# The operands of a Strassen-like second layer for the next pair of token blocks: made in the first layer and read back from DRAM

## The chip, the core and the metric

The kernel runs on one core of a Trainium2 chip. A core has a matrix engine (TensorE, PE in the profile; its weight loads are PEld), three engines for elementwise work (VectorE is DVE, ScalarE is ACT, GpSimd is POOL) and a queue that issues DMAs (SyncE, SP). Each engine runs its instructions in order and waits at semaphores for the others. The metric is the device time of one execution in microseconds; smaller is better. The profiled times come from one execution that was recorded.

## What is computed

Attention without softmax, an RMS norm over each head, a first feed-forward layer with a maximum of three products, an RMS norm, and a gated second layer:

```python
kv = np.einsum('bhsd,bhse->bhde', k, v)
out = np.einsum('bhsd,bhde->bhse', q, kv)              # 8 x 8 heads x 576 x 64
x = (out / rms(out) * g_norm) -> (4608, 512)
h = np.maximum(np.maximum(x @ w1, x @ w2), x @ w3)     # 512 -> 768
x = h @ w_out                                          # 768 -> 512
xn = x / rms(x) * rms_g
g = xn @ w_gate                                        # 512 -> 1536
return (silu(g) * (xn @ w_val)) @ w_out2               # 1536 -> 512
```

All in fp32, and the weights come as 64-bit floats.

## The kernel before

*Precision.* A product of fp32 matrices is made of three matmuls (`mm3`, `prod3`): each operand is split into a high part (an ACT copy to the matrix engine's fp32 format) and a low part (the difference, on DVE or POOL), and high x high, high x low and low x high are added up. Every operand that PE reads therefore costs one ACT and one DVE or POOL operation first.

*First layer.* The 4608 tokens are 9 blocks `t` of 512. The loop over `t` = 2 to 8 runs six steps `j`, one for each 128 of the 768 columns: `do_p` makes three products into PSUM; ACT copies the first ("s"), DVE takes the maximum with the second ("s", line 323) and the third ("h", line 327), and the result is split ("hs"). `do_o` adds it into the four accumulators of the output. Between the products, `mid` calls `pump`, which moves on the conversion of the weights from 64-bit floats: `store_pair` converts, sums, splits and stores the second layer's weights in DRAM ("ws" to "wd"). The attention of the next block ("ao", "pk", "pt") also runs in these steps. After a block, `end1` copies the accumulators to four tiles "y", and `end1_rest`, moved on by one call of `flush` a step, norms them and stores them in DRAM as `xn_d[t]`. All temporaries of 512 columns come from one pool "t" of 8 buffers (`tmp`).

*Second layer.* One block (`NB`) is done in the plain way (`do_gv`, "the gated part", six matmuls by two halves for each of 12 steps). The other eight form four pairs `n`, and a pair is multiplied by a scheme with 7 products in place of 8 (as Strassen and Winograd do it). It has 3 phases of 4 units each (`run_unit`; a unit is the gate, i = 0, or the value, i = 1, for 256 columns), and at a phase's end `down` multiplies by the output weights. The products m = 1, 2, 3 take blocks of the input as they are; m = 5, 6, 4, 7 take sums and differences of blocks. Each of the 7 has two halves k, so a pair needs 14 split operands, "xo".

`build_x` makes them: it starts in the last unit of a pair's third phase for the next pair and goes on through `down`, one step in every second `slot`. The raw blocks "xr" are loaded a phase earlier (`load_x`). The differences run on DVE (`diff`, line 491), the high parts on ACT (line 483), the low parts in turn on POOL, POOL and DVE (line 486). `consume` takes a product out of PSUM: the sum "c" on DVE, then the sigmoid "sg" on ACT and its product "sl" on DVE, two ticks later (`defer`; `tick` follows each product). Weights come through `Ring`, four loads ahead, on SP; the buffers of operands and weights ("u", 38) are shared.

The order of work on each engine is that of the program text, with the deferred calls at their ticks; no scheduler moves it.

Of the kernel before, what the change touches and what calls it, by code (L numbers as in the profile page):

```python
# [34 lines left out]
def tile_kernel(ctx: ExitStack, tc, qT, k, v, gcol, w1, w2, w3, wo, wg, wv, wo2, rmsg, out):  # L35
# [89 lines left out]
    def store_pair(i, jp):  # L125
# [27 lines left out]
        for n, src in enumerate((quarters[0], c0, c1, quarters[1])):  # L153
            g = unit([P, 2, 2, 256], F32R, "ws")
            for o, (dst, sv) in enumerate([(g, src)] if n in (1, 2) or i < 2 else [(g[:, k], src[k]) for k in range(2)]):
                if isinstance(sv, tuple):
                    sv = (t0, t1)[n // 2]
                hi, lo = (dst[:, 0], dst[:, 1]) if len(dst.shape) == 3 else (dst[:, :, 0], dst[:, :, 1])
                nc.scalar.activation(hi, sv, AF.Copy)
                nc.vector.tensor_tensor(lo, sv, f32(hi), ALU.subtract)  # L160
            d = w_d[i, jp, n] = dp.tile([P, 2, 2, 256], F32, name="wd", tag=f"wd{i}_{jp}_{n}")
            nc.sync.dma_start(d, f32(g))
            yield
# [5 lines left out]

    def pump(n=1):  # L170
        for _ in range(n):
            for g in list(flight):
                if next(g, 0) == 0:
                    flight.remove(g)
            if todo and len(flight) < most[0]:
                start(todo[0])
# [230 lines left out]
    def end1_rest(t, y, q, w):  # L407
# [20 lines left out]
        for c in range(KC):  # L428
            nc.sync.dma_start(xn_d[t][c * P:(c + 1) * P, :], y[c])

# [42 lines left out]
    def load_x(t):  # L473
        raw = xp.tile([P, KC, 2, TB], F32, tag="x", name="xr")
        for k in range(2):
            nc.sync.dma_start(raw[:, :, k], xn_d[t + k].rearrange("(c p) n -> p c n", p=P))
        XR.append(raw)

    n_lo = [0]

    def split_b(key, src):
        x = unit([P, 2, TB], F32R, "xo")
        nc.scalar.activation(x[:, 0], src, AF.Copy)  # L483
        n_lo[0] += 1
        eng = nc.vector if n_lo[0] % 3 == 0 else nc.gpsimd
        eng.tensor_tensor(x[:, 1], src, f32(x[:, 0]), ALU.subtract)  # L486
        XO[key] = x

    def diff(x, y, name):
        t = tmp(name)  # L490
        nc.vector.tensor_tensor(t, x, y, ALU.subtract)  # L491
        return t

    def build_x():
        raw = XR.pop(0)
        b11, b12, b21, b22 = ([raw[:, 2 * r + k, c] for k in range(2)] for r in range(2) for c in range(2))
        t1, t2 = {}, {}
        for k in range(2):
            split_b((1, k), b11[k])
        yield  # L500
        for k in range(2):
            t1[k] = diff(b12[k], b11[k], "t1")
            split_b((5, k), t1[k])
        yield
        for k in range(2):
            split_b((2, k), b21[k])
        yield
        for k in range(2):
            t2[k] = diff(b22[k], t1[k], "t2")
            split_b((6, k), t2[k])  # L510
        yield
        for k in range(2):
            split_b((3, k), b22[k])
        yield
        for k in range(2):
            split_b((7, k), diff(b22[k], b12[k], "t3"))
        yield
        for k in range(2):
            split_b((4, k), diff(b21[k], t2[k], "t4"))
# [95 lines left out]
    def hidden(jp, c, h):  # L615

        HQ[jp, c] = h

        def part(m, src):
            HO[jp, m] = split_h(src, "ho")  # L620

        if c == 0:
            defer(lambda: part(1, h))
        elif c == 1:
            t1 = T[jp, 1] = diff(h, HQ[jp, 0], "t1")
            defer(lambda: part(5, t1), 1)
        elif c == 3:
            t2 = T[jp, 2] = diff(h, T.pop((jp, 1)), "t2")
            t3 = diff(h, HQ[jp, 1], "t3")
            defer(lambda: part(6, t2))  # L630
            defer(lambda: part(3, h), 5)
            defer(lambda: part(7, t3), 7)
        else:
            t4 = diff(h, T.pop((jp, 2)), "t4")
            defer(lambda: part(2, h), 1)
            defer(lambda: part(4, t4), 5)


    def consume(u, c, p, s=None):
        n, jp, i = u["key"]  # L640
        src = p if s is None else add(p, s, tmp("c"))
        if i == 0:
            sg = tmp("sg")
            nc.scalar.activation(sg, src, AF.Sigmoid)  # L644

            def mult():
                sl = small("sl")
                nc.vector.tensor_tensor(sl, src, sg, ALU.mult)
                SL[c] = sl

            defer(mult)
# [55 lines left out]
    def down(n, ph, xs):  # L707
# [25 lines left out]
        def put(d, c, p, alone=False):  # L733
            o = place(d, c)
            if ph + 1 == NPH:
# [3 lines left out]
                nc.sync.dma_start(out[r:r + P, q:q + TB], t)  # L739
# [36 lines left out]
        for d in range(2):  # L776
            prod_down(d, ph, 4, acc[d][0])
            put(d, 2, acc[d][0], True)
            slot()
        if xs is not None:  # L780
            for _ in xs:
                pass

    with tc.manual_schedule():
# [13 lines left out]
        for i in range(2):  # L798
            z = unit([P, 2, NP, P], F32, "kvbd")
            nc.gpsimd.memset(z, 0.0)  # L800
            kvb += [z[:, 0], z[:, 1]]
# [39 lines left out]
        def kv_upto(need, ahead=True):  # L841
            while n_kv[0] <= min(need, B - 1):
                n = n_kv[0]
                do_kv(n, kvb[n % 4])
# [121 lines left out]
        for j in range(J2):  # L966
# [8 lines left out]
            do_gv(NB, j, none)  # L975
            if 3 <= j <= 5:
                flush()
# [9 lines left out]
            if j == 2:  # L987
                xb = build_x()
# [5 lines left out]
        for _ in xb:  # L994
            pass
        for n in range(NPAIR):
            for ph in range(NPH):
                more = n + 1 < NPAIR
                xs = None
                for jp in range(PPH * ph, PPH * (ph + 1)):  # L1000
                    for i in range(2):
                        if i == 1 and jp + 1 == PPH * (ph + 1):
                            load_down(ph)
                            if ph + 1 == NPH and more:
                                xs = build_x()
# [40 lines left out]
```

## Time and profile before

| | |
|---|---|
| median of 3 runs | 1582.43 us (1580.74 to 1583.18) |
| the profiled execution's own time | 1582.51 us |
| span of the profiled execution | 1580.4 us |
| PE busy | 1500.0 us, 95% of the span |
| DVE, ACT, POOL busy | 953.1, 580.1, 490.5 us (60%, 37%, 31%) |
| mean granted clock of PE | 0.978 of full speed |
| moved by DMA | 278 MB, 176 GB/s over the span |

The first layer takes up about 700 us, the gated part lasts until about 835 us, and each of the 12 phases of the second layer is some 58 us of matmuls. A row of the timeline gives the start, the duration, the engine, the source line, the operation with its output and inputs, and in brackets how long the engine had been idle before and for whom. Matmuls overlap: a matmul of 512 columns is listed with about 390 ns while six of them start within 1.36 us. A granted clock of 1.00 is 2.4 GHz, 0.50 is 1.2 GHz.

### The profile page before, as it was taken

The page shows a single profiled execution, that of the slowest core. Times are in us where ns is not written, and L with a number is a line of the kernel's source. Part 1 is how long each engine was busy: PE and PEld are TensorE (multiplying, and loading weights), DVE is VectorE, ACT ScalarE, POOL GpSimd, SP SyncE. Part 2 cuts the span into 40 slices and gives each one's busy share as a digit, 9 for nine tenths or more (in the row PEclk, how much of TensorE's full clock was granted, in tenths as well). Part 3 has the DMA queues.
Part 4 walks back from the last instruction along what each step waited for, and adds up shares of the span by engine and source line. Part 5 has one row for each costly group of instructions (what it writes and reads, how often), then busy time and mean ns, then how long its engine had stood idle before and what let it go on. Part 6 is the DMA issues. An engine that isn't in the chain of part 4 may idle for free. (4 is left out here: it accounts for less than half of the span.)

```text
span 1580.4 us, 19695 instructions
## 1 busy us (share of the span) xinstructions
PE 1500.0 (95%) x7200; PEld 1230.8 (78%) x7200; DVE 953.1 (60%) x1404; ACT 580.1 (37%) x1027; POOL 490.5 (31%) x375
## 2 busy tenths in 40 slices
PE   5899999999989999999999999799988999899998
PEld 5787878787778878888887878588776887678887
DVE  4875565656666567642525476764676655865656
ACT  3443333434343434322324334243243432434422
POOL 2543222212222222211422242532343422544323
PEclk8999999999999999999999999899998999999999
DMA  9322437354724353446428474184543854456442
GB/s 305 121 67 81 119 115 260 127 169 151 255 98 160 135 199 135 173 149 260 178 86 318 162 270 170 60 326 180 220 160 121 308 200 157 161 206 246 161 169 104
DMA packets 117343, 278.11 MB, mean 176 GB/s; under 512 B 10496, under 2 KB 41216, under 8 KB 117248
## 3 DMA queue, kind: packets, MB, share of 16 engines
q1 hardware_dynamic: 117248, 276.87, 48.6%
q8 instruction: 57, 0.93, 0.2%
q14 instruction: 38, 0.31, 0.1%
HBM read 220.20 MB, written 56.62 MB: 175 GB/s over the span
## 5 line engine op out<-in xcount | busy, mean ns | idle before, releaser
L292 PE MATMUL p<-x,w 128*128 128x512 f32 (+1 forms) x652 | 262.2, 402 | 17.6 <-DVE h L327 12.8
L293 PE MATMUL p<-x,w 128*128 128x512 f32 (+1 forms) x652 | 257.7, 395 | 0.4 <-DVE x L285 0.3
L294 PE MATMUL p<-x,w 128*128 128x512 f32 (+1 forms) x652 | 257.2, 394 | 0.0
L582 PE MATMUL ua<-xo,w 128*128 128x512 f32 x864 | 215.5, 392 | 8.0 <-ACT s L659 8.0
L582 PEld LDWEIGHTS ua<-xo,w 128*128 128x128 f32 x864 | 161.9, 188 | 46.5 <-ACT s L659 13.1
L311 POOL TENSOR_TENSOR ho<-sl,ho 128x512 fp32r<-128x512 f32 x72 | 100.3, 1401 | 308.3 <-issue 163.2
L311 POOL TENSOR_TENSOR hs<-h,hs 128x512 fp32r<-128x512 f32 x54 | 69.6, 1289 | 383.9 <-ACT hs L310 305.7
L311 POOL TENSOR_TENSOR ho<-t,ho 128x512 fp32r<-128x512 f32 x96 | 131.5, 1374 | 135.7 <-ACT ho L310 123.6
L292 PEld LDWEIGHTS p<-x,w 128*128 128x128 f32 x652 | 125.7, 193 | 46.4 <-DVE h L327 14.2
L582 PE MATMUL ub<-xo,w 128*128 128x512 f32 x576 | 146.3, 389 | 0.0
L294 PEld LDWEIGHTS p<-x,w 128*128 128x128 f32 x652 | 125.5, 192 | 26.4
L293 PEld LDWEIGHTS p<-x,w 128*128 128x128 f32 x652 | 125.7, 193 | 25.5 <-DVE x L285 1.0
L582 PEld LDWEIGHTS ub<-xo,w 128*128 128x128 f32 x576 | 108.1, 188 | 22.7
L582 PE MATMUL da<-ho,wd 128*128 128x512 f32 x432 | 109.8, 398 | 4.9 <-DVE op L612 3.4
L310 ACT ACTIVATE hs<-h 128x512 fp32r<-128x512 f32 x54 | 34.1, 632 | 193.8 <-DVE h L327 184.4
L659 ACT ACTIVATE s<-ua 128x512 f32<-128x512 f32 x96 | 57.2, 596 | 123.1 <-PE ua L582 122.8
L582 PEld LDWEIGHTS da<-ho,wd 128*128 128x128 f32 x432 | 82.8, 193 | 24.5 <-DVE op L612 4.7
L310 ACT ACTIVATE ho<-t 128x512 fp32r<-128x512 f32 x96 | 59.3, 627 | 100.8 <-DVE t L491 100.8
L256 POOL TENSOR_TENSOR rs<-ms,mhalf 128x8 f32<-128x8 f32 x36 | 61.9, 1725 | 109.0 <-DVE ms L254 106.1
L644 ACT ACTIVATE sg<-c 128x512 f32<-128x512 f32 x72 | 45.5, 632 | 108.3 <-DVE c L612 108.3
L292 PE MATMUL acc<-hs,w 128*128 128x512 f32 x216 | 84.9, 393 | 0.0
L582 PE MATMUL db<-ho,wd 128*128 128x512 f32 x288 | 74.7, 398 | 10.4 <-ACT ho L310 6.5
(133 smaller groups left out, 2733.8 us busy)
## 6 DMA issues: line engine op xcount, KB each, us to landing
w<-wd SPq DMA_DIRECT2D x180, 512.0 KB, 7.7
wd<-ws SPq DMA_DIRECT2D x72, 512.0 KB, 3.1
wd<-wd SPq DMA_DIRECT2D x72, 512.0 KB, 6.5
wq<-wd SPq DMA_DIRECT2D x72, 256.0 KB, 7.7
raw<-in_w SPq DMA_DIRECT2D x18, 512.0 KB, 8.2
q<-in_qT SPq DMA_DIRECT2D x18, 512.0 KB, 6.0
raw<-in_wo SPq DMA_DIRECT2D x18, 512.0 KB, 6.3
xn<-y SPq DMA_DIRECT2D x36, 256.0 KB, 3.1
```

The costliest lines, as they stand in the source:

```text
L256: nc.gpsimd.tensor_tensor(rs, ms, mhalf.to_broadcast([P, H]), ALU.pow)
L292: nc.tensor.matmul(o, ah, bh, start=first, stop=False)
L293: nc.tensor.matmul(o, ah, bl, start=False, stop=False)
L294: nc.tensor.matmul(o, al, bh, start=False, stop=last)
L310: nc.scalar.activation(hs[:, 0], h, AF.Copy)
L311: nc.gpsimd.tensor_tensor(hs[:, 1], h, f32(hs[:, 0]), ALU.subtract)
L582: nc.tensor.matmul(o, aa, bb, start=first and q == 0, stop=last and q == 2, skip_group_check=True)
L644: nc.scalar.activation(sg, src, AF.Sigmoid)
L659: nc.scalar.activation(t, p, AF.Copy)
```

## The change

For each pair, `pair_sums` makes the eight operands that are sums (m = 5, 6, 4, 7, two halves) out of the tiles "y" of the second block of the pair, which are still there, and the first block's blocks read back from `xn_d[t - 1]`. It splits them and stores high and low part in DRAM ("td"). It is queued in `side` when an even block has been stored and moved on twice by each `pump` (and by the gated part's steps). `build_x` then loads these eight and makes only the six others, with all low parts on POOL; `load_x` reads three of four quarters. In `consume` the sigmoid is a deferred call, and so is the store of an output in `put`. A weight's store in `store_pair` comes a step later, the block matrices "kvbd" have two buffers in place of four, and the last `flush` calls come a step earlier.

```diff
@@ store_pair, pump
+            yield
             d = w_d[i, jp, n] = dp.tile([P, 2, 2, 256], F32, name="wd", tag=f"wd{i}_{jp}_{n}")
             nc.sync.dma_start(d, f32(g))
-            yield
...
+    def aside():
+        if side and next(side[0], 0) == 0:
+            side.pop(0)
+
     def pump(n=1):
         for _ in range(n):
+            aside()
+            aside()
             for g in list(flight):
@@ end1_rest
             nc.sync.dma_start(xn_d[t][c * P:(c + 1) * P, :], y[c])
+        if t and t % 2 == 0:
+            side.append(pair_sums(t, y))
@@
+    def pair_sums(t, y):
+
+        n = t // 2 - 1
+
+        def put(m, k, src):
+            hi = tmp("th").bitcast(F32R)
+            nc.scalar.activation(hi, src, AF.Copy)
+            nc.vector.tensor_tensor(src.bitcast(F32R), src, f32(hi), ALU.subtract)
+            return m, k, hi, src
+
+        def store(m, k, hi, lo):
+            d = t_d[n, m, k] = dp.tile([P, 2, TB], F32, name="td", tag=f"td{n}_{m}_{k}")
+            nc.sync.dma_start(d[:, 0], f32(hi))
+            nc.sync.dma_start(d[:, 1], lo)
+
+        for k in range(2):
+            b12, b22 = y[k], y[2 + k]
+            b11, b21 = tmp("b11"), tmp("b21")
+            for b, c in ((b11, k), (b21, 2 + k)):
+                nc.sync.dma_start(b, xn_d[t - 1][c * P:(c + 1) * P, :])
+            yield
+            yield
+            t1 = diff(b12, b11, b11)
+            t2 = diff(b22, t1, tmp("t2"))
+            yield
+            p1 = put(5, k, t1)
+            t4 = diff(b21, t2, b21)
+            yield
+            store(*p1)
+            p1 = put(6, k, t2)
+            yield
+            store(*p1)
+            p1 = put(4, k, t4)
+            t3 = diff(b22, b12, tmp("t3"))
+            yield
+            store(*p1)
+            p1 = put(7, k, t3)
+            yield
+            store(*p1)
...
+    def build_x(n):
+
         raw = XR.pop(0)
-        b11, b12, b21, b22 = ([raw[:, 2 * r + k, c] for k in range(2)] for r in range(2) for c in range(2))
...
+        for m, r in ((1, 0), (5, None), (2, 1), (6, None), (3, 2), (7, None), (4, None)):
+            for k in range(2):
+                x = unit([P, 2, TB], F32R, "xo")
+                if r is None:
+                    nc.sync.dma_start(f32(x), t_d[n, m, k])
+                else:
+                    nc.scalar.activation(x[:, 0], raw[:, r, k], AF.Copy)
+                    nc.gpsimd.tensor_tensor(x[:, 1], raw[:, r, k], f32(x[:, 0]), ALU.subtract)
+                XO[m, k] = x
+            yield
@@ consume, put, down
-            sg = tmp("sg")
-            nc.scalar.activation(sg, src, AF.Sigmoid)
-
-            def mult():
+            def gate():
+                sg = tmp("sg")
+                nc.scalar.activation(sg, src, AF.Sigmoid)
+                defer(lambda: mult(sg))
+
+            def mult(sg):
                 sl = small("sl")
                 nc.vector.tensor_tensor(sl, src, sg, ALU.mult)
                 SL[c] = sl
 
-            defer(mult)
+            if s is None:
+                gate()
+            else:
+                defer(gate, 1)
...
-                nc.sync.dma_start(out[r:r + P, q:q + TB], t)
+                defer(lambda: nc.sync.dma_start(out[r:r + P, q:q + TB], t), 1)
...
+        tick()
```

What this does to the order on the engines, at three places. First DVE in the first layer, t = 3, from the attention's "xn" in step j = 3 to the maximum "s" of j = 4. Before ("wt" are weights in conversion):

```order
L261 TENSOR_TENSOR xn<-po,rs 128x512
L107 TENSOR_SCALAR wt<-wt 128x512
L108 SCALAR_TENSOR_TENSOR wt<-raw,wt 128x512
L109 ISA wt<-wt 128x1024
L99 TENSOR_SCALAR wt<-raw 128x512
L323 TENSOR_TENSOR s_2888<-p_2875,s_2866 128x512
```

After; "b" and "t" are the differences of `pair_sums` (L486), "th" their high parts (L496 is the low part):

```order
L269 TENSOR_TENSOR xn<-po,rs 128x512
L486 TENSOR_TENSOR b_2846<-y,b_2846 128x512
L486 TENSOR_TENSOR t_2871<-y,b_2846 128x512
L496 TENSOR_TENSOR b_2846<-b_2846,th 128x512
L486 TENSOR_TENSOR b_2847<-b_2847,t_2871 128x512
L107 TENSOR_SCALAR wt<-wt 128x512
L108 SCALAR_TENSOR_TENSOR wt<-raw,wt 128x512
L109 ISA wt<-wt 128x1024
L99 TENSOR_SCALAR wt<-raw 128x512
L331 TENSOR_TENSOR s_2897<-p_2884,s_2868 128x512
```

Four of the sixteen operations stand ahead of this "s"; the others follow in the same way up to the end of j = 5.

Second, DVE in the last units of the first pair's third phase, before, from the last "t" of one value unit to the first sum of the last unit:

```order
L491 TENSOR_TENSOR t_8135<-sl,t_8061 128x512
L648 TENSOR_TENSOR sl<-c,sg 128x512
L612 TENSOR_TENSOR c<-ua,s_8088 128x512
L648 TENSOR_TENSOR sl<-c,sg 128x512
L486 TENSOR_TENSOR xo<-xr,xo 128x512
L612 TENSOR_TENSOR c<-uc,s_8182 128x512
```

and after:

```order
L486 TENSOR_TENSOR t_8383<-sl,t_8309 128x512
L641 TENSOR_TENSOR c<-ua,s_8336 128x512
L679 TENSOR_TENSOR sl<-c,sg 128x512 x2
L641 TENSOR_TENSOR c<-uc,s_8430 128x512
L688 TENSOR_TENSOR sl<-c,sl 128x512
```

The sum "c<-ua", on which the next sigmoid waits, has moved ahead of one product "sl", and the subtraction of "xo" has left DVE.

Third, SP at the end of that phase. Before, "w" and "wq" are weights of the next units, "wd" and the "wq" of line 562 those of `down`, and "out" the output stores:

```order
L565 DMA wd<-wd 128x1024 x6
L562 DMA wq<-wd 128x512 x2
L546 DMA w<-wd 128x1024 x3
L543 DMA wq<-wd 128x512
L546 DMA w<-wd 128x1024
L739 DMA out<-o 128x512 x8
```

and after, with the loads of operands from "td" between them:

```order
L594 DMA wd<-wd 128x1024 x6
L591 DMA wq<-wd 128x512 x2
L575 DMA w<-wd 128x1024 x2
L543 DMA xo<-td 128x1024 x2
L575 DMA w<-wd 128x1024
L572 DMA wq<-wd 128x512
L575 DMA w<-wd 128x1024
L543 DMA xo<-td 128x1024 x2
L773 DMA out<-o 128x512 x2
L543 DMA xo<-td 128x1024 x2
L773 DMA out<-o 128x512
L543 DMA xo<-td 128x1024 x2
```

Five more output stores follow. The eight loads stand between weights and stores, in four pairs.

## Rows read from the trace of the kernel before

**Rows 1.** The page, part 1: busy us, share of the span, instructions of each engine.
```profile
PE 1500.0 (95%) x7200; PEld 1230.8 (78%) x7200; DVE 953.1 (60%) x1404; ACT 580.1 (37%) x1027; POOL 490.5 (31%) x375
```

**Rows 2.** Waits of PE: line, for whom, us in total, times, longest us.
```profile
PE p L292 <- DVE h L327: 12.8, 7, 2.8
...
PE da L582 <- DVE o L612: 8.7, 3, 4.1
PE ua L582 <- ACT s L659: 8.0, 12, 0.7
```

**Rows 3.** Timeline of the first build (start, us, engine, line, operation, idle before).
```profile
982.97 1.65 PE L582 MATMUL ua<-xo,w 128*128 128x512 f32 x6 [0.67 <-ACT s L659]
...
993.63 0.63 ACT L310 ACTIVATE ho<-t 128x512 fp32r<-128x512 f32 x1 [3.19 <-DVE t L491]
...
994.31 0.79 PE L582 MATMUL db<-ho,wd 128*128 128x512 f32 x1 [3.56 <-ACT ho L310]
...
997.12 2.76 PE L582 MATMUL ua<-xo,wq 128*128 128x512 f32 x6
...
1018.63 5.49 PE L582 MATMUL da<-ho,wq 128*128 128x512 f32 x12 [3.24 <-DVE o L612]
...
1023.91 1.70 PE L582 MATMUL ua<-xo,w 128*128 128x512 f32 x6
```

**Rows 4.** Windows there: stretch, its us, busy us (instructions), clock, DMA share, GB/s.
```profile
984.00:994.00 10.00, 6.75 (x30) 5.25 (x28) 9.13 (x10) 3.72 (x7) 6.40 (x4) 0.98 0.11 43
994.00:1000.00 6.00, 4.69 (x10) 3.42 (x11) 5.01 (x8) 2.42 (x5) 4.37 (x4) 0.50 0.01 3
```

**Rows 5.** Groups of instructions, DVE differences: busy us, mean ns, idle before.
```profile
L491 DVE TENSOR_TENSOR t<-sl 128x512 f32<-128x512 f32 x48 | 34.8, 725 | 1.7
...
L491 DVE TENSOR_TENSOR t<-xr 128x512 f32<-128x512 f32 x16 | 20.4, 1301 | 0.0
```

**Rows 6.** Timeline of the last phase, which builds nothing.
```profile
1549.85 1.67 PE L582 MATMUL ua<-xo,w 128*128 128x512 f32 x6 [0.67 <-ACT s L659]
...
1562.44 2.54 POOL L311 TENSOR_TENSOR ho<-sl,ho 128x512 fp32r<-128x512 f32 x2 [1.70 <-PE db L582]
...
1573.89 2.88 PE L582 MATMUL da<-ho,wq 128*128 128x512 f32 x12
```

**Rows 7.** Timeline of PE in the second and third build.
```profile
1173.28 1.66 PE L582 MATMUL ua<-xo,w 128*128 128x512 f32 x6 [0.67 <-ACT s L659]
...
1214.79 1.82 PE L582 MATMUL ua<-xo,w 128*128 128x512 f32 x6
...
1364.28 1.66 PE L582 MATMUL ua<-xo,w 128*128 128x512 f32 x6 [0.67 <-ACT s L659]
...
1372.07 0.73 PE L582 MATMUL da<-ho,wd 128*128 128x512 f32 x2 [1.15 <-POOL ho L311]
...
1400.67 1.52 PE L582 MATMUL ua<-xo,w 128*128 128x512 f32 x6
```

**Rows 8.** DMA issues: count, KB each, median us from issue to landing.
```profile
w<-wd SPq DMA_DIRECT2D x180, 512.0 KB, 7.7
```

**Rows 9.** Timeline of DVE and ACT ahead of the wait at 982.97.
```profile
979.33 1.77 DVE L648 TENSOR_TENSOR sl<-c,sg 128x512 f32<-128x512 f32 x1
...
981.03 0.68 DVE L612 TENSOR_TENSOR c<-ua,s 128x512 f32<-128x512 f32 x1
...
981.80 0.63 ACT L644 ACTIVATE sg<-c 128x512 f32<-128x512 f32 x1 [3.54 <-DVE c L612]
982.34 0.58 ACT L659 ACTIVATE s<-ua 128x512 f32<-128x512 f32 x1
```

**Rows 10.** Windows in the first layer and the gated part: PE, PEld, DVE, ACT, POOL.
```profile
333.00:366.00 33.00, 33.00 (x217) 27.49 (x216) 18.12 (x35) 11.85 (x23) 4.66 (x5) 1.00 0.59 205
...
743.00:821.00 78.00, 78.00 (x346) 64.48 (x345) 33.00 (x43) 20.64 (x36) 26.53 (x20) 1.00 0.45 174
```

**Rows 11.** Timeline of PE in the first layer, a stop for "h".
```profile
396.77 0.79 PE L292 MATMUL p<-x,w 128*128 128x512 f32 x1 [2.76 <-DVE h L327]
```

**Rows 12.** A window of the first layer with a full DMA.
```profile
348.00:358.00 10.00, 10.00 (x45) 8.27 (x45) 3.95 (x7) 2.63 (x6) 0.00 (x0) 1.00 1.01 335
```

**Rows 13.** Waits of the queue SP.
```profile
SPq L546 <- PE da L582: 118.9, 24, 14.7
```

More of the change, by code (lines that the diff above doesn't have):

```diff
@@ L168, in start @@
         flight.append(g)
+    side = []
+    def aside():
+        if side and next(side[0], 0) == 0:
+            side.pop(0)
     def pump(n=1):
         for _ in range(n):
+            aside()
+            aside()
             for g in list(flight):
@@ L471, in tile_kernel @@
     HO = {}
[L473 to L487, printed above, removed]
@@ L489, in diff @@
-    def diff(x, y, name):
-        t = tmp(name)
+    t_d = {}
+    def diff(x, y, t):
         nc.vector.tensor_tensor(t, x, y, ALU.subtract)
         return t
-    def build_x():
-        raw = XR.pop(0)
-        b11, b12, b21, b22 = ([raw[:, 2 * r + k, c] for k in range(2)] for r in range(2) for c in range(2))
[L497 to L519, printed above, removed]
+    def pair_sums(t, y):
[33 more added lines that the diff above has]
+            store(*p1)
@@ new lines, in load_x @@
+    def load_x(t):
+        raw = xp.tile([P, 3, 2, TB], F32, tag="x", name="xr")
+        nc.sync.dma_start(raw[:, 0], xn_d[t][:2 * P].rearrange("(c p) n -> p c n", p=P))
+        for k in range(2):
+            nc.sync.dma_start(raw[:, 1 + k], xn_d[t + k][2 * P:].rearrange("(c p) n -> p c n", p=P))
+        XR.append(raw)
+    def build_x(n):
+        raw = XR.pop(0)
+        for m, r in ((1, 0), (5, None), (2, 1), (6, None), (3, 2), (7, None), (4, None)):
+            for k in range(2):
+                x = unit([P, 2, TB], F32R, "xo")
[6 more added lines that the diff above has]
+            yield
@@ L624, in hidden @@
         elif c == 1:
-            t1 = T[jp, 1] = diff(h, HQ[jp, 0], "t1")
+            t1 = T[jp, 1] = diff(h, HQ[jp, 0], tmp("t1"))
             defer(lambda: part(5, t1), 1)
         elif c == 3:
-            t2 = T[jp, 2] = diff(h, T.pop((jp, 1)), "t2")
-            t3 = diff(h, HQ[jp, 1], "t3")
+            t2 = T[jp, 2] = diff(h, T.pop((jp, 1)), tmp("t2"))
+            t3 = diff(h, HQ[jp, 1], tmp("t3"))
             defer(lambda: part(6, t2))
@@ L633, in hidden @@
         else:
-            t4 = diff(h, T.pop((jp, 2)), "t4")
+            t4 = diff(h, T.pop((jp, 2)), tmp("t4"))
             defer(lambda: part(2, h), 1)
@@ L797, in tile_kernel @@
         kvb = []
[L798 to L801, printed above, removed]
+        z = unit([P, 2, NP, P], F32, "kvbd")
+        nc.gpsimd.memset(z, 0.0)
+        kvb += [z[:, 0], z[:, 1]]
         nc.sync.dma_start(gc, gcol)
@@ L843, in kv_upto @@
                 n = n_kv[0]
-                do_kv(n, kvb[n % 4])
+                do_kv(n, kvb[n % 2])
                 n_kv[0] += 1
@@ L974, in tile_kernel @@
                 wr.load(1)
-            do_gv(NB, j, none)
-            if 3 <= j <= 5:
+            do_gv(NB, j, aside)
+            aside()
+            if 2 <= j <= 4:
                 flush()
@@ L987, in tile_kernel @@
             if j == 2:
-                xb = build_x()
+                xb = build_x(0)
             if j > 2 and xb is not None:
@@ L995, in tile_kernel @@
             pass
+        while side:
+            aside()
         for n in range(NPAIR):
@@ L1004, in tile_kernel @@
                             if ph + 1 == NPH and more:
-                                xs = build_x()
+                                xs = build_x(n + 1)
                         run_unit(n, jp, i, xs)
```

## The prediction

> **What bounds the kernel now.** I read the page first: the matrix engine (PE) is busy for 95% of the span, DVE for 60%, ACT for 37%, POOL for 31% [rows 1]. So PE is the bound, and a change that leaves its 7200 matmuls as they are can only take back time in which PE waits, or add to it. The waits of PE come next [rows 2]. Three families matter: 8.0 us in 12 waits for a copy "s" of ACT, at most 0.7 us each, one in every phase of the second layer; waits of "da" and "db" in the three phases that also build the operands of the next pair, of which the one for DVE "o" is the largest; and 12.8 us of "p" for DVE "h" in the first layer, into which the change puts work.
>
> Then the timeline of the first of the three building phases [rows 3]: PE stops for 3.56 us, later for 3.24 us, and after each stop it is slow: six matmuls take 2.76 us, where twelve take 2.88 us at full clock; the granted clock of 994 to 1000 us is 0.50, that is 1.2 instead of 2.4 GHz [rows 4]. So a stop costs more than its length. DVE is the late one: busy for 9.13 of the 10 us before and in the first long stop [rows 4], and ACT, whose split PE waits for, waited 3.19 us itself for a DVE difference [rows 3]. A difference of the build costs DVE 1.301 us on the mean, where POOL works beside it, one of the unit's own 0.725 us [rows 5].
>
> **The change part by part.**
>
> *The builds lose their DVE work.* Each of the three late builds has 8 differences and 4 or 5 of its 14 subtractions on DVE, and 8 of its 14 ACT copies belong to sums. All these go, and 8 loads of 512 KB from DRAM replace them. I price the stretch against the one phase with the same products and stores and no build, the last of the program: from its wait for "s" at 1549.85 to the end of its last products, 1573.89 + 2.88, it takes 26.92 us [rows 6]. The builds take, up to the next pair's first product, 1023.91 - 982.97 = 40.94 us [rows 3], 1214.79 - 1173.28 = 41.51 and 1400.67 - 1364.28 = 36.39 us [rows 7]. Over 26.92 that is 14.02 + 14.59 + 9.47 = **38.1 us** to be had, the low clock's share included.
>
> Not all of it, since six ACT copies and six POOL subtractions stay in each build. Two stand on POOL ahead of the splits that the first "da" needs; the third build already has that order, and "da" waited 1.15 us for POOL there [rows 7]. Two more stand ahead of the two splits that "dc" needs. In the phase without a build POOL is idle for 1.70 us before those, and two such operations take 2.54 us [rows 6], so "dc" comes 0.8 us later. Bounds: nothing, or both pairs in full, 2 x 2.54 = 5.1 us a build. I take 0.7 (POOL is faster once DVE's differences are gone) and 0.8, so **4.5 us** of the three stay.
>
> *The loads* stand on SP, in order, among the weights of the next pair and the output stores. A load that waits for a free buffer holds what is behind it. A 512 KB load of weights lands 7.7 us after its issue [rows 8]. The two last pairs of loads (m = 7 and 4) go out during the last four groups of twelve matmuls, some 11 us before the pair ends, and the next pair wants m = 7 only five products, about 7 us, after its start, m = 4 a unit later. DMA is busy for 11% before the first stop [rows 4]. I cost the loads at nothing, hidden behind those products; the third rival is the case without that cover.
>
> *The gates.* The sigmoid is deferred by one tick, but that tick follows at once, so on ACT it keeps its place. What moves is DVE's product "sl", by one matrix product, since its two ticks are now counted from the sigmoid: in the phase's last but one unit "c<-ua" stands ahead of a "sl<-c,sg" instead of behind it. What that is worth: the product takes 1.77 us, only then comes "c", "sg" has left ACT idle for 3.54 us, and the copy that PE waits for stands behind "sg" [rows 9]. With "c" first, "sg" runs some 1.7 us earlier, more than the 0.67 us of the wait. All twelve should go: **8.0 us** [rows 2], or nothing if it is the order on ACT that makes them.
>
> *The sums made early.* Per pair there are 8 differences and 8 subtractions on DVE, 8 copies on ACT, 4 loads and 16 stores of 256 KB on SP, within about 33 us: for three pairs in the steps j = 3 to 5 of t = 3, 5 and 7, for the last pair in the gated part. There PE has no gap in 743 to 821 us and DVE is busy for 33.00 of 78 us [rows 10], part of it the old first build, which goes; I cost this pair at nothing. In 333 to 366 us, the place in t = 3 (t = 5 and 7 repeat it), PE has no gap either and DVE is busy for 18.12 of 33 us [rows 10]. Sixteen operations at 0.725 us [rows 5] are 11.6 us; 14.9 us are free. By the sum they fit, but DVE is in order, and its "s" and "h" come behind them. Where DVE is late today, PE stops: 2.76 us for "h" before 396.77 [rows 11], and six slow matmuls after a stop add 2.76 - 1.52 = 1.2 us [rows 3, 7]. Bounds per pair: nothing, or two such stops, 8 us. DVE would be 90% busy and the loads come one pump ahead of the first difference, so I take one stop, 4.0 us: **12 us** for three.
>
> The stores meet a full DMA: 348 to 358 us moves 335 GB/s at a share of 1.01 [rows 12]. By that rate some 2.6 MB more there is 8 us longer. Behind it wait the next weights and the 8 buffers "t", which "s" and "h" use too; this is in the upper bound.
>
> Here a page speaks against the change. The Trainium skill, GPSIMD Engine Reference, Specifications, says that GpSimd's SBUF interfaces are shared with VectorE and contend with its instructions on two SBUF inputs, which all sixteen have; the second rival is that case, priced from rows.
>
> *The rest*: half the buffers for the block matrices, a weight's store one step later, the output stores behind the tick. None moves a matmul, and PE waits for none of them today. Nothing.
>
> **The sum** is made against the profiled execution's 1582.51 us (its span 1580.4 and 2.1 around it), 0.1 us from the median 1582.43: 1582.5 - 38.1 + 4.5 - 8.0 + 12 = 1552.9, **1553 us**.
>
> **The rivals.** *First*, POOL and ACT take DVE's place in the builds: 5.1 us each instead of 1.5, and 2 us each for the clock that falls (twelve slow matmuls add 5.49 - 2.88 = 2.6, six 1.2 [rows 3, 6]): 21 instead of 4.5, 1570 us. For it: "da" waited for POOL already [rows 7]. Against: the longest stops are DVE's [rows 2, 3]. 0.15.
>
> *Second*, the early sums run at the build's 1.301 us: 20.8 us against 14.9 free [rows 5, 10], 5.9 over, and 1.2 for the clock: 7 us a pair, 21 for three instead of 12, 1562 us. For it: the same operations take that long in the builds. Against: POOL is busy for only 4.66 of those 33 us [rows 10]. 0.2.
>
> *Third, and slower*: the loads wait on SP for buffers that PE's last products free, and two in turn, 2 x 7.7 = 15.4 us, stand ahead of the next pair: 46 us in three builds, 1582.5 - 38.1 - 8.0 + 12 + 46 = 1594 us. It decides from (38.1 + 8.0 - 12) / 3 = 11.4 us a build. For it: SP waits 118.9 us in 24 cases for "da" today, up to 14.7 us [rows 13]. Against: PE waits for no load in the second layer today. 0.05.
>
> *Fourth*, the gates don't do what they say: the sigmoid keeps its place and so do the waits, 1561 us. 0.08. That the parts cancel has 0.03.
>
> **How the numbers follow.** The forecast has 0.49, for 1544 to 1559 us. The range's low end is all gains at no price, 1536, raised to 1538, since some price is near certain; its high end takes in the first rival, 1570. About 0.2%, 3 us, is what a measurement can tell from no change. Faster: 0.49 + 0.15 + 0.2 + 0.08 = 0.92; within: 0.03; slower: 0.05.
>
> **What would show it.** After the change: no wait of "ua" for ACT "s"; the three stretches at 27 to 30 us instead of 36 to 42, with no difference from "xr" on DVE and a granted clock of 1.00; PE's waits in t = 3, 5 and 7 up by some 9 us, with DVE near full there; no wait of PE for a load of "xo". I am wrong if "s" or "h" waits for the store of a sum, if the stretches stay above 32 us, or if PE stops in a pair's first units.

## The result: 1543.0 us, and the profile after

The changed kernel takes 1542.98 us, median of 4 runs (1541.62 to 1543.52), beside 1582.60 for the kernel before (1580.74 to 1583.18): a ratio of 0.975, 95% interval 0.9733 to 0.9767. That is 39.6 us less; the forecast was 29.6 less, and its range, 1538 to 1570, holds the time. The profiled execution took 1542.86 us, its span 1541.1.

The page first, against [rows 1]: busy us, share of the span and instructions of each engine, and among the DMA issues the new loads (count, KB each, median us from issue to landing).

```profile
PE 1486.0 (96%) x7200; PEld 1226.3 (80%) x7200; DVE 938.5 (61%) x1418; ACT 576.3 (37%) x1027; POOL 460.9 (30%) x360
...
xo<-td SPq DMA_DIRECT2D x32, 512.0 KB, 7.3
```

PE has the same 7200 matmuls. DVE has done hardly less (938.5 for 953.1 us): its work has moved, not gone. The waits of PE, against [rows 2] (line, for whom, us in total, times, longest us):

```profile
PE p L300 <- DVE h L335: 9.8, 7, 2.0
...
PE dc L611 <- POOL ho L319: 5.5, 8, 1.1
...
PE db L611 <- POOL ho L319: 3.8, 3, 1.3
```

The family "ua" for ACT "s" (8.0 us in 12) is gone, and so are "da" for DVE "o" and "op" and "db" for ACT "ho". POOL's splits are what PE still waits for in the builds. The timeline of PE in the three builds, against [rows 3] and [rows 7]; each stretch begins with a "ua" and ends with the next pair's first product:

```profile
984.90 1.52 PE L611 MATMUL ua<-xo,w 128*128 128x512 f32 x6
...
994.05 0.74 PE L611 MATMUL db<-ho,wd 128*128 128x512 f32 x2 [1.27 <-POOL ho L319]
994.63 1.56 PE L611 MATMUL ua<-xo,wq 128*128 128x512 f32 x6
...
1000.84 2.11 PE L611 MATMUL dc<-ho,wd 128*128 128x512 f32 x8 [1.01 <-POOL ho L319]
...
1013.66 1.52 PE L611 MATMUL ua<-xo,w 128*128 128x512 f32 x6
...
1159.94 1.52 PE L611 MATMUL ua<-xo,w 128*128 128x512 f32 x6
...
1188.70 1.52 PE L611 MATMUL ua<-xo,w 128*128 128x512 f32 x6
...
1335.00 1.52 PE L611 MATMUL ua<-xo,w 128*128 128x512 f32 x6
...
1363.81 1.52 PE L611 MATMUL ua<-xo,w 128*128 128x512 f32 x6
```

The stretches are 28.76, 28.76 and 28.81 us instead of 40.94, 41.51 and 36.39. The stops are shorter, and no group behind them runs slowly: six matmuls take 1.56 us at 994.63, where they took 2.76. The windows there, against [rows 4], have the clock at 1.00 (after the busy times of PE, PEld, DVE, ACT, POOL: clock, DMA share, GB/s):

```profile
985.00:995.00 10.00, 8.73 (x39) 6.91 (x38) 8.59 (x9) 3.67 (x7) 7.66 (x5) 1.00 0.83 331
995.00:1001.00 6.00, 4.99 (x23) 3.78 (x22) 4.61 (x8) 4.48 (x9) 5.71 (x5) 1.00 0.01 3
```

To split the 39.6 us I take the start of the first product "ua" of the second layer as the border. The rows of "ua" in the kernel before, then in the one after (median ns, first and last start):

```profile
L582 PE MATMUL ua<-xo,w x864: 387/389/628, 833.8 to 1555.2; 128*128 128x512 f32 x173
```

```profile
L611 PE MATMUL ua<-xo,w x864: 389/389/389, 838.6 to 1515.3; 128*128 128x512 f32 x173
```

The longest "ua" was 628 ns and is 389 now: there is no slow matmul left among them. Up to the border the change costs 838.6 - 833.8 = 4.8 us; behind it, it gains (1580.4 - 833.8) - (1541.1 - 838.6) = 44.1 us.

| part | forecast us | measured us | how it is read |
|---|---|---|---|
| builds | -38.1 + 4.5 = -33.6 | -32.5 | three stretches: 12.18 + 12.75 + 7.58 |
| gates | -8.0 | -11.6 | the rest of the second layer, 44.1 - 32.5 |
| up to the border (first layer, gated part) | +12 | +4.8 | starts of the first "ua" |
| around the span | 0 | -0.3 | 2.1 before, 1.8 after |
| sum | -29.6 | -39.6 | |

The +4.8 is the difference of two single executions, and executions of one kernel already differ by up to 5 us before the block t = 3 begins. The experiments below therefore also count from the first product "acc" of t = 3. From there to the border five traces that have the changed kernel's first layer take 545.0 to 545.8 us; the kernel before takes 539.5, and a second trace with its first layer 541.7. So the change costs 3.3 to 6.3 us there. Behind the border the changed kernel takes 702.4 and 702.5 us in two traces, so the 44.1 is steadier.

### The profile page after: what moved, and what is told of

Same layout as the page of the kernel before. It is cut to its first block, busy times and chain, and to the rows that moved or that the text cites. A ratio compares the mean times of both kernels' runs of the same rounds, so it can differ in the third digit from the quotient of the medians.

```text
span 1541.1 us, 19959 instructions
## 1 busy us (share of the span) xinstructions
PE 1486.0 (96%) x7200; PEld 1226.3 (80%) x7200; DVE 938.5 (61%) x1418; ACT 576.3 (37%) x1027; POOL 460.9 (30%) x360
## 4 chain that ended last, share of the span: by engine, by line
PE 50%; POOL 3%; issue 2%; ACT 1%; DVE 0%; POOLq 0%; DVEq 0%
PE ua L611 15%; PE ub L611 8%; PE da L611 8%; PE uc L611 4%; PE db L611 4%; POOL ho L319 2%; PE dc L611 2%; PE acc L301 1%; PE acc L300 1%; PE acc L302 1%; PE pv L302 1%; PE p L302 1%; PE pg L302 1%; PE pv L300 1%; PE pg L300 1%
## 5 line engine op out<-in xcount | busy, mean ns | idle before, releaser
L611 PEld LDWEIGHTS ua<-xo,w 128*128 128x128 f32 x864 | 162.2, 188 | 33.6
L319 POOL TENSOR_TENSOR ho<-t,ho 128x512 fp32r<-128x512 f32 x96 | 125.5, 1311 | 117.9 <-ACT ho L318 110.6
L611 PE MATMUL da<-ho,wd 128*128 128x512 f32 x432 | 105.8, 389 | 0.0
L300 PE MATMUL acc<-hs,w 128*128 128x512 f32 x216 | 84.9, 393 | 0.0
L641 DVE TENSOR_TENSOR c<-uc,s 128x512 f32<-128x512 f32 x48 | 33.1, 689 | 84.7 <-PE uc L611 84.7
L301 PE MATMUL acc<-hs,w 128*128 128x512 f32 x216 | 84.2, 390 | 0.5 <-POOL hs L319 0.5
```

The costliest lines, as they stand in the source:

```text
L300: nc.tensor.matmul(o, ah, bh, start=first, stop=False)
L301: nc.tensor.matmul(o, ah, bl, start=False, stop=False)
L319: nc.gpsimd.tensor_tensor(hs[:, 1], h, f32(hs[:, 0]), ALU.subtract)
L611: nc.tensor.matmul(o, aa, bb, start=first and q == 0, stop=last and q == 2, skip_group_check=True)
L641: nc.vector.tensor_tensor(t, p, s, ALU.add)
```

## The experiments

Each was timed in rounds beside the kernel before. The changed kernel, run once more among them, gave 1542.58 us (ratio 0.9746, 0.9727 to 0.9765). Executions of one kernel lie up to 7 us apart here, so a difference of medians under some 2 us is not read as one. Part of the scatter arises ahead of t = 3, whose first "acc" starts anywhere between 290.6 and 295.5 us in the traces.

### The gates alone, and the gates undone

```diff
-            sg = tmp("sg")
-            nc.scalar.activation(sg, src, AF.Sigmoid)
+            def gate():
+                sg = tmp("sg")
+                nc.scalar.activation(sg, src, AF.Sigmoid)
+                defer(lambda: mult(sg))
...
-            defer(mult)
+            if s is None:
+                gate()
+            else:
+                defer(gate, 1)
```

> The kernel before with only the gate change: the sigmoid deferred by one tick, its product counted from the sigmoid. Theory (the order on DVE made the waits, since the sum c stood behind a product): the 12 waits of ua for ACT s, 8.0 us in the kernel before, are gone, and the time falls by 8.0 from 1582.4 to about 1574.5 us; nothing else moves. Rival (it is the order on ACT that makes the waits, and what removed them in the changed kernel is the emptier DVE): the waits stay and the time stays at 1582 us.

> The changed kernel with the gates as before. Theory (the gates are worth 8.0 us by themselves, whatever the builds do): the 12 waits of ua for ACT s come back at about 0.67 us each, and the time rises from 1543.0 to about 1551 us. Rival (the builds' DVE work made them): no such waits, 1543 us.

The kernel before with this edit took 1571.25 us beside 1583.97 (ratio 0.9921, 0.9905 to 0.9937): 12.7 us less. The changed kernel without it took 1555.20 (0.9817, 0.9801 to 0.9833): 12.2 us more than 1542.98. In the first the 12 waits are gone, in the second they are back, 8.0 us in 12. So the order on DVE made them, the builds had no part in it, and both rivals fall. But each time 12 us came or went, not 8. From the border to the end, where the traces are steady, it is 746.6 - 734.3 = 12.3 us in the first and 715.8 - 702.5 = 13.3 in the second. The timeline of PE in a phase without a build shows why; first with the gates undone, then the changed kernel:

```profile
926.94 1.52 PE L611 MATMUL uc<-xo,w 128*128 128x512 f32 x6
929.14 1.67 PE L611 MATMUL ua<-xo,w 128*128 128x512 f32 x6 [0.67 <-ACT s L688]
930.64 1.55 PE L611 MATMUL ub<-xo,w 128*128 128x512 f32 x6
932.03 1.52 PE L611 MATMUL ua<-xo,wq 128*128 128x512 f32 x6
```

```profile
925.66 1.52 PE L611 MATMUL uc<-xo,w 128*128 128x512 f32 x6
927.02 1.52 PE L611 MATMUL ua<-xo,w 128*128 128x512 f32 x6
928.38 1.52 PE L611 MATMUL ub<-xo,w 128*128 128x512 f32 x6
```

Undisturbed, a group of six starts 1.36 us after the one before it, though its row is 1.52 us long: the rows overlap by 0.16. With the stop, "ua" starts 2.20 us after "uc" (0.84 late), "ub" 1.50 after "ua" (0.14 late) and the next 1.39 after that (0.03 late). A stop that reads 0.67 us of idle time delays PE by 1.01 us; twelve like it would be 12.1. The Trainium skill, Perfetto Trace Analysis, Tensor Engine Instruction (MATMUL, LD_WEIGHTS), says that the end of a matmul in a profile is an estimate and not observed. The rows agree in so far as idle time counted from such an end misses 0.16 us of each stop.

What moved on DVE and ACT is seen ahead of that same product of the changed kernel, against [rows 9]:

```profile
924.19 0.68 DVE L641 TENSOR_TENSOR c<-ua,s 128x512 f32<-128x512 f32 x1
924.79 1.79 DVE L679 TENSOR_TENSOR sl<-c,sg 128x512 f32<-128x512 f32 x2
...
924.96 0.64 ACT L674 ACTIVATE sg<-c 128x512 f32<-128x512 f32 x1 [1.51 <-DVE c L641]
925.50 0.58 ACT L693 ACTIVATE s<-ua 128x512 f32<-128x512 f32 x1
```

"c" stands ahead of the products now, ACT waits 1.51 instead of 3.54 us for it, and "s" is done at 926.08, before PE wants it at 927.02.

### The early sums left out, and made but not stored

```diff
-        if t and t % 2 == 0:
-            side.append(pair_sums(t, y))
```

```diff
-            d = t_d[n, m, k] = dp.tile([P, 2, TB], F32, ...)
-            nc.sync.dma_start(d[:, 0], f32(hi))
-            nc.sync.dma_start(d[:, 1], lo)
+            pass
```

> The changed kernel without the sums made in the first layer: their loads, differences, splits and stores are left out, and the operands of the sums are loaded from stored weights of the same size instead, so the result is of wrong data. It prices the whole of the early work. The trace of the changed kernel puts the first layer 4.8 us later than before, net; theory: about 5 us come back, 1538 us, most of it in t = 3. Rival (the prediction's term of 12 us was right and the rest of the first layer gained 7 us elsewhere): 1531 us.

> The changed kernel with the sums loaded, computed and split in the first layer, but not stored; their operands are loaded from stored weights of the same size, so the result is of wrong data. It separates the price of the work on DVE and ACT from that of the stores. Theory (the price is paid through a full DMA: in t = 3 a split of ACT waits 6.1 us for the store of weights, and PE behind it): the time is that without any sums, within 1 us of 1538 us, and those waits are gone. Rival (the sixteen DVE operations in order ahead of s and h, as the prediction costed it): the time stays at 1543 us, and the PE waits in t = 3 stay.

Without the sums 1535.19 us (ratio 0.969, 0.9674 to 0.9706), with sums made but not stored 1536.70 (0.97, 0.9684 to 0.9716). Behind the border both take as long as the changed kernel, 702.5 and 702.2 us, so the whole difference lies ahead of it. The rows of "ua" of the two (spans 1534.6 and 1534.9):

```profile
L609 PE MATMUL ua<-xo,w x864: 389/389/389, 832.1 to 1508.8; 128*128 128x512 f32 x173
```

```profile
L609 PE MATMUL ua<-xo,w x864: 388/389/401, 832.7 to 1509.5; 128*128 128x512 f32 x173
```

Taken from the start of the program the early work costs 838.6 - 832.1 = 6.5 us, but the execution without the sums was nearly 2 us late before any sum is made. These are the first "acc" of t = 3, in the changed kernel, without the sums, and with the sums not stored:

```profile
293.36 0.40 PE L300 MATMUL acc<-hs,w 128*128 128x512 f32 x1
```

```profile
295.26 0.40 PE L300 MATMUL acc<-hs,w 128*128 128x512 f32 x1
```

```profile
293.21 0.40 PE L300 MATMUL acc<-hs,w 128*128 128x512 f32 x1
```

From there to the border it is 545.2, 536.8 and 539.5 us. So the early work costs 8.4 us (8.2 to 9.0 over the five traces): 5.7 for the stores, and 2.7 for the loads, differences, splits and copies, 48 operations of DVE in the three pairs among them. The medians give 7.8, 6.3 and 1.5. The 2.7 comes from one trace on each side and isn't clear of noise; the 5.7 is. Over the five traces the pair of t = 3 costs 3.1 to 4.0 us of it (from the first "acc" of t = 3 to that of t = 4, 81.8 to 82.7 us instead of 78.7).

The rest of the change, which I had put at nothing, gains there: the kernel before takes 539.5 and 541.7 us where the changed kernel without the sums takes 536.8, so 2.7 to 4.9 us. One stop of PE that goes is 1.67 us for "s" at 299.36 in the kernel before. Which part of the change removes it was not tried: the block matrices' two buffers and the earlier `flush` calls were not undone by themselves.

In t = 3 the stores make these windows (us 355 to 385), first of the changed kernel, then of the one that doesn't store:

```profile
355.00:365.00 10.00, 8.95 (x43) 7.02 (x41) 4.10 (x6) 3.43 (x7) 1.28 (x1) 1.00 1.02 398
365.00:375.00 10.00, 8.46 (x36) 6.68 (x36) 5.80 (x11) 7.28 (x15) 1.29 (x1) 1.00 1.01 356
375.00:385.00 10.00, 6.58 (x30) 5.21 (x31) 7.34 (x14) 2.48 (x5) 2.94 (x3) 0.87 0.43 138
```

```profile
355.00:365.00 10.00, 10.00 (x50) 8.43 (x49) 5.90 (x9) 5.88 (x14) 2.59 (x2) 1.00 0.60 205
365.00:375.00 10.00, 10.00 (x47) 8.22 (x46) 6.24 (x11) 5.32 (x11) 2.27 (x2) 1.00 0.84 280
375.00:385.00 10.00, 8.06 (x33) 6.35 (x32) 7.88 (x13) 3.87 (x7) 2.30 (x2) 0.83 0.00 1
```

DMA is full for 20 us in the changed kernel, and PE loses 1.05 and 1.54 us there while DVE is busy for half the time. From 325 to 400 us a store of block weights lands after 6.6 us instead of 3.9, and ACT's split "hs" waits for one; the first row is of the changed kernel (DMA issues), the second the kernel without the stores, the third ACT's timeline in the changed kernel:

```profile
wd<-ws SPq DMA_DIRECT2D x8, 512.0 KB, 6.6
```

```profile
wd<-ws SPq DMA_DIRECT2D x9, 512.0 KB, 3.9
```

```profile
358.61 0.63 ACT L318 ACTIVATE hs<-h 128x512 fp32r<-128x512 f32 x1 [6.10 <-DMA wd<-ws]
```

### Three ways to move the stores

A pause between the two halves of a pair's sums; the stores on ACT's queue; and the pair of t = 3 made 11 pumps later (this one with the low parts on DVE, below).

```diff
+            if k == 0:
+                for _ in range(4):
+                    yield
```

```diff
-            nc.sync.dma_start(d[:, 0], f32(hi))
-            nc.sync.dma_start(d[:, 1], lo)
+            nc.scalar.dma_start(d[:, 0], f32(hi))
+            nc.scalar.dma_start(d[:, 1], lo)
```

```diff
+        if y is None:
+            for _ in range(22):
+                yield
...
-            side.append(pair_sums(t, y))
+            side.append(pair_sums(t, None if t == 2 else y))
```

> The changed kernel with a pause of two pumps, some 9 us, between the first half (k = 0) and the second half (k = 1) of a pair's sums, so that their stores are spread over more time and, in t = 3, half of them comes behind the stretch with the full DMA. Theory (the price of the stores, 5.9 us, is that of DMA traffic on top of a full DMA): about half of the 4.3 us of t = 3 is gone, 1541 us, and ACT's wait of 6.1 us for the store of block weights is shorter. Rival (the price is SP's order, whatever the traffic): 1543 us, and the wait stays.

> The changed kernel with the stores of the sums issued on ACT's queue instead of SP's. The traffic is the same; SP is no longer held while it waits for a split (94.8 us in 20 waits, up to 12.6 us, in the changed kernel), with the key and value loads and the stores of block weights behind it. Theory of the order on SP: the 5.9 us of the stores go, 1537 us, and no split of ACT waits for a store of block weights. Rival of the traffic: the DMA is as full, the wait of some 6 us stays, 1543 us. Third: ACT, in order, stops for a low part that DVE has not made, and s and hs come later: over 1545 us.

> The kernel with the build's low parts on DVE, in which in addition the sums of the pair made in t = 3 start 11 pumps later, some 50 us, when DMA is idle in the trace of the changed kernel (0.00 from 380 to 400 us); their blocks b12 and b22 are read back from DRAM for it, 1 MB more. Theory (in t = 3 the price is the stores of the sums on top of a full DMA, which make a store of weights take 6.6 us instead of 4.0): the waits of 360 to 381 us go, the first layer is some 4 us shorter, and the time is 1538 us. Rival (PE has no slack for the DVE work in the later place, where s and h are late already in the kernel before): the waits come there, and the time is 1542 us or more.

None helps. The pause gave 1548.19 us (0.977, 0.9744 to 0.9795): "hs" still waits 5.0 us for a store of block weights, and PE's "pr" now 4.4 us for "s", where it is 1.6 in the changed kernel. My theory of half the price was wrong; the wait stays, as the rival had it, but the time is 5 us over the rival's. On ACT's queue it is 1546.71 (0.9758, 0.9736 to 0.9781): ACT's wait for "wd" is gone, so SP's order did make that wait, but DMA is as full (a share of 1.04 from 355 to 375 us) and PE stops in the same place for "s" and "h". The time is the third forecast's, over 1545 us, and so is one sign of it: from 325 to 400 us the copies "th" wait 11.9 us for DVE in place of 6.6. ACT is held in SP's stead, so this run can't part the order from the traffic. Made later, 1544.08 (0.9763, 0.9750 to 0.9777), with these windows:

```profile
365.00:375.00 10.00, 10.00 (x48) 8.22 (x47) 6.52 (x12) 4.15 (x8) 2.26 (x2) 1.00 0.49 170
...
385.00:395.00 10.00, 5.68 (x38) 4.13 (x36) 9.83 (x19) 4.21 (x8) 1.64 (x2) 1.00 0.69 252
395.00:405.00 10.00, 9.23 (x34) 7.55 (x35) 9.90 (x19) 4.37 (x8) 3.34 (x2) 0.83 0.41 143
```

PE is full at 365 to 375 us again, but DVE is busy for 9.83 and 9.90 of 10 us in the later place, and PE loses 4.32 and 0.77 us there. So t = 3 has a place where DMA is full and one where DVE is; the change has the one, this kernel the other. From the first "acc" of t = 3 to that of t = 4 it takes 78.7 us, as without the sums; the price comes back one block later. It is level with the kernel with the low parts on DVE (1541.91) and not below it, as the rival had it. That the stores make the price is shown; how much of it is traffic and how much the order of what waits behind it stays open.

### Stores at once

```diff
-            yield
             d = w_d[i, jp, n] = dp.tile([P, 2, 2, 256], F32, ...)
             nc.sync.dma_start(d, f32(g))
+            yield
...
-                defer(lambda: nc.sync.dma_start(out[r:r + P, q:q + TB], t), 1)
+                nc.sync.dma_start(out[r:r + P, q:q + TB], t)
```

> The changed kernel with the third part of the change undone: a block matrix's store goes to SP right behind its split, an output store right behind its sum, each a step earlier than in the changed kernel. Theory (the prediction's: no wait of PE hangs on them): within 2 us of 1543 us, first layer and second layer alike. Rival (SP, in order, is held by the earlier wait for the split or for o, and the loads behind it come late): over 1546 us, in the first layer by PE waits behind weights, in the second by waits of the next pair's first products.

1542.51 us (0.9733, 0.9714 to 0.9752) beside 1542.58: these two moves are worth nothing that can be measured, as forecast.

### The loads held twice as long

```diff
                     nc.sync.dma_start(f32(x), t_d[n, m, k])
+                    nc.sync.dma_start(f32(x), t_d[n, m, k])
```

> The changed kernel with each of the 32 loads of split sums issued twice into the same buffer, so that SP is held for one more landing, about 7.3 us, per load, and the loads of a build take 58 us longer on SP. It asks how far the loads are from the path. Theory (they are hidden with room, since PE waits for none of them): up to two landings per pair of loads are covered, and the time rises by less than 10 us, below 1553 us. Rival (the third one of the prediction, loads ahead of the next pair's weights): 2 x 7.3 us or more per build, three builds, over 44 us, 1587 us or more, with PE waits for loads of xo or w at a pair's start.

1601.45 us (1.0113, 1.0090 to 1.0136), 58.9 more than the changed kernel; the theory of a wide margin is wrong, and the rival's size is about right. The rows: PE's waits; SP's; and in the first build the timelines of ACT and PE.

```profile
PE ua L612 <- ACT s L694: 42.4, 3, 15.2
```

```profile
SPq L544 <- DMA xo<-td: 165.3, 32, 10.0
```

```profile
1043.14 0.60 ACT L694 ACTIVATE s<-ua 128x512 f32<-128x512 f32 x1 [9.25 <-DMA out<-o]
...
1043.79 4.77 PE L612 MATMUL ua<-xo,w 128*128 128x512 f32 x12 [13.34 <-ACT s L694]
```

PE doesn't wait for a load even here. SP, in order, holds the output stores behind the loads; the stored sums "o" keep their buffers, which are those of "s" too; ACT can't copy, and PE stops. SP is held 165.3 / 32 = 5.2 us per load, 41 per build. From the border to the end it is 1600.4 - 848.4 = 752.0 instead of 702.5 us, 16.5 a build. By these rows, as an estimate, some 25 of the 41 us are covered. The other 848.4 - 838.6 = 9.8 us are lost ahead of the border, where the first pair's eight loads stand in the gated part: PE stops there once, 5.86 us, for ACT's "gs".

### POOL's low parts on DVE

```diff
-                    nc.gpsimd.tensor_tensor(x[:, 1], raw[:, r, k], f32(x[:, 0]), ALU.subtract)
+                    nc.vector.tensor_tensor(x[:, 1], raw[:, r, k], f32(x[:, 0]), ALU.subtract)
```

```diff
-            HO[jp, m] = split_h(src, "ho")
+            HO[jp, m] = split_h(src, "ho", nc.vector if m == 2 else nc.gpsimd)
```

> The changed kernel with the six low-part subtractions of a build on DVE instead of POOL. Theory (those left on POOL stand ahead of the split of ho and make the waits of db, 1.27 us, and half of those of dc, 1.04 us, in the three builds): db's waits are gone, dc's fall to the 0.5 us of the phases without a build, and with the slow matmuls around a stop that is some 2.4 us a build, 7 us in all: 1536 us. Rival (DVE, in order, comes as late as POOL, since it stands behind c and o): the waits stay, for DVE xo or POOL ho, 1543 us.

> As the one before, and also the low part of the hidden product m = 2 on DVE instead of POOL, in all 12 phases. Theory (the dc wait of 0.5 us that is left in every phase is POOL's, which has two splits of ho in a row there, 2.5 us): all waits of dc go, 0.76 us from start to start in each of 12 phases, so some 9 us less than the kernel before this one: 1527 us. Rival (the wait only moves to the low part of the m = 4 split or to DVE): within 2 us of the kernel before this one.

The first gave 1541.91 us (0.9737, 0.9718 to 0.9756), no measurable gain where 7 us was expected: the waits shrink, "db" to 0.8 and "dc" to 0.9 us, and don't go. The second edit, on top of it, gave 1545.21 (0.9763, 0.9744 to 0.9782): "dc" is nearly free, but "db" waits in all 12 phases, 9.0 us. The wait moved, as the rival had it. From the border to the end, which is steady to some 0.4 us, the first takes 700.9 us and the second 704.9, beside 702.4 and 702.5: a gain of 1.5 and a loss of 2.5.

Why the waits don't go is in DVE and POOL of the first, ahead of "db" at 991.35:

```profile
986.45 0.69 DVE L688 TENSOR_TENSOR sl<-c,sl 128x512 f32<-128x512 f32 x1
987.18 1.66 DVE L486 TENSOR_TENSOR t<-sl 128x512 f32<-128x512 f32 x1
...
991.77 0.68 DVE L486 TENSOR_TENSOR t<-sl 128x512 f32<-128x512 f32 x1
992.37 0.68 DVE L679 TENSOR_TENSOR sl<-ua,sg 128x512 f32<-128x512 f32 x1
```

```profile
986.56 1.73 POOL L319 TENSOR_TENSOR ho<-sl,ho 128x512 fp32r<-128x512 f32 x1 [1.29 <-ACT ho L318]
...
992.59 1.30 POOL L319 TENSOR_TENSOR ho<-t,ho 128x512 fp32r<-128x512 f32 x1 [1.29 <-ACT ho L318]
```

The same two operations in the changed kernel, ahead of its own wait of "db" at 994.05:

```profile
989.88 1.67 DVE L486 TENSOR_TENSOR t<-sl 128x512 f32<-128x512 f32 x1
```

```profile
989.26 1.74 POOL L319 TENSOR_TENSOR ho<-sl,ho 128x512 fp32r<-128x512 f32 x1
```

A difference that takes 0.68 us alone takes 1.66 while POOL subtracts, and POOL's 1.30 becomes 1.73; "db" hangs on a chain of such operations on both. Each is longer by about what the other still had to run when it started: DVE by 0.98, of POOL's 1.11 us, and POOL by 0.43, of the 0.58 of the product "sl" before. The product "sl<-ua,sg", with one input in PSUM, isn't slowed beside POOL: 0.68, and POOL 1.30. The pair is as slow in the changed kernel, so the move from POOL to DVE neither made this nor took it away, and it is why the rest of the wait stays. In the second kernel it comes to the phases without a build too: ahead of "db" at 935.83 the products "sl" take 1.65 and 1.51 us, where the changed kernel has 0.99 and 0.88, and POOL's split 1.72 for 1.29. The Trainium skill, GPSIMD Engine Reference, Specifications, which the prediction weighed, says that the SBUF interfaces of GpSimd are shared with VectorE and contended for with its instructions on two SBUF inputs; these rows agree.

No kernel that was tried and makes and stores the sums beats the changed one's median by more than can be measured.

## Why the prediction was right, and where its terms were off

**The bound and the sign.** PE was the bound, only its waits could be had, and they were. No "ua" waits for "s", the stretches are 29 us, the clock is 1.00 in them and PE waits for no load of "xo": four of the signs that the prediction named. Of its signs of being wrong none came for "s" or "h"; POOL's low part "hs" does wait once for the store of a sum, 6.6 us in t = 5, and PE waits for no "hs" there.

**The builds** were sized well: 32.5 for 33.6 us. Pricing a stretch against the same products without the build took in the stops, what follows each stop, and the low clock at once. (Its 26.92 us runs to the end of the last row and not to a next start, which by the overlap of rows is 0.16 us too much.) What stays is POOL, as the prediction's bounds had it, though at "db" and "dc", not "da", and 1.9 us instead of 1.5 a build.

**The gates** had the right mechanism and the wrong size: 8.0 forecast, 11.6 to 13.3 measured. The term was the idle time of the waits table. The prediction says itself that a stop costs more than its length, but used it only for stops with a low clock; a stop of 0.67 us at full clock delays PE by 1.01.

**The first layer** is where the sum was furthest off: 12 forecast, 4.8 measured. It is two terms. The early sums cost 8.4 us, and the rest of the change, put at nothing since PE waited for none of it, gained 2.7 to 4.9. For the sums I took one DVE stop of 4.0 us per pair. The operations of the pairs in t = 3, 5 and 7 ran at 0.68 to 0.71 us, but for one in each pair of 1.36 to 1.41, and in the stretch of [rows 10] DVE was busy for 24.51 of 33 us, not 90% (four of the sixteen operations had run before it):

```profile
333.00:366.00 33.00, 31.91 (x213) 26.25 (x212) 24.51 (x45) 12.28 (x24) 2.58 (x2) 1.00 0.80 283
743.00:821.00 78.00, 78.00 (x346) 64.50 (x345) 28.95 (x42) 22.08 (x39) 21.77 (x17) 1.00 0.74 278
```

"h" costs PE 9.8 us now and 12.8 before, so the sign that I had named, waits up by 9 us with DVE near full, did not show. Most of the price, 5.7 of 8.4 us, came with the stores, in the full DMA of [rows 12], which the prediction had counted in its upper bound only. So this term had the wrong mechanism for the most part, and that its size came as near as it did is luck. The second row, the gated part with the fourth pair, has PE without a gap, as forecast.

**The rivals.** The first (POOL and ACT in DVE's place) is right in kind, at 1.9 instead of 7 us a build. The second (the sums at 1.301 us) is not borne out in the first layer, where POOL is busy for 2.58 of 33 us; the slowdown it rests on is real in the builds. The third needs SP held much longer than the change holds it, and then comes by way of the output stores' buffers, not as a wait for loads. The fourth falls to both runs on the gates. The forecast of 1553 missed by 10 us because the gates, by 3.6 us, and the first layer, by 7.2, erred to the same side.

## What to carry to other kernels

Price a stop of the matrix engine from the starts of the groups around it, against the same groups undisturbed: here a wait read as 0.67 us cost 1.01, half as much again. When work moves into an earlier stage, look for what is full there, engine by engine and DMA too, at the very place: within 40 us of t = 3 one place had no DMA left and the next no DVE. And a load that nobody waits for may still matter through what stands behind it on its queue, and through the buffers which that holds.

## What the runs showed of the hardware that I had not expected

Two engines that are both far from full hold each other up where both read two SBUF inputs: beside POOL, DVE's 0.68 us becomes 1.66, and POOL's 1.30 becomes 1.73, each longer by about what the other still had to run, while a DVE product with one input in PSUM stays at 0.68. Work taken off POOL and put on DVE left that as it was and gained 1.5 us of the 7 expected. And moving 16 stores a pair from SP's to ACT's queue took away the wait behind SP and no time: 1546.71 us for 1542.98.

The same stop can be followed by a low clock or not. In the first layer, the same program in two traces, PE waits 2.69 us for "h" in both; from 555 to 565 us, around that stop, the granted clock is 1.00 in the kernel before and 0.66 in the kernel with the gates alone.
